# A list-scheduled kernel whose planner supposes later landings and longer hand-overs

## The chip, the cores and the metric

The kernel runs on one core of a Trainium2 chip. The metric is device time in microseconds (us) of one execution. The core has five instruction streams: TensorE (PE, with its weight loads PEld), VectorE (DVE), ScalarE (ACT), GpSimd (POOL) and SyncE (SP), which here issues all loads and transposes by DMA. Engines meet through semaphores only.

## What is computed

Sparse attention, then a feed-forward layer with a softmax-weighted activation and a layer norm. In the reference's terms, cut to what matters:

```python
# q, k, v: 8 batches, 8 heads, 576 positions, 64 wide
scores = (q @ k.T) / 8                       # heads 0-3: the last 32 positions; heads 4-7: every 32nd position
attn = softmax(where(mask, scores, -1e9))
x = (attn @ v) laid out as 4608 tokens x 512
h = x @ w_in                                 # 512 -> 1024
solu = h * softmax(h)
ln = (solu - mean) / sqrt(var + 1e-6) * g_ln
out = ln @ w_out                             # 1024 -> 512
```

Attention inputs are float32. For the large matmuls the kernel splits each operand into two float16 parts, a high and a low one, and adds three products.

## The kernel before

**Tiles and stages.** A *unit* (`unit`, line 322) is one of five pieces of a batch's attention: two for the strided heads, three for the local ones; 40 in all. Its steps are: scores into `s_ps` on TensorE (L341, L346); row maximum, subtraction, exponential, row sum and reciprocal on VectorE and ScalarE (L352 to L361); normalisation on GpSimd (L364, tile `t`); high and low parts on ScalarE and VectorE (L370, L371, tile `p`); a DMA transpose to `pt` (L373); the product with v into `x_ps` on TensorE (L394); and the two parts of x, `xhi` and `xlo` (L410, L411), written to a ring that holds two batches.

An *ff tile* (`ff`, line 415) is 128 tokens through the feed-forward layer; 36 in all. Its steps are: two halves of the first matmul, `g1` (L452 to L454, 12 matmuls each, one PSUM bank each of `h_ps`); the maximum `st` (L459, L460); the exponential `e` (L461); the product `u` (L463) and its mean (L466); the squares (L467); GpSimd's small norms (L471 to L481); the two parts of `c` (L484, L485); a DMA transpose to `ct` (L488); two halves of the second matmul, `g2` (L492 to L494), into `o_ps`; and the scaling and the store (L500, L501).

`h_ps` has three banks. Tile n uses banks 0 and 1, then the next tile 0 and 2, then the next 1 and 2, so one half of the next tile can start while the tile before it still holds its own two banks:

```python
banks, halves = (((0, 1), (0, 1)), ((0, 2), (1, 0)), ((1, 2), (0, 1)))[n % 3]
hv, o, O = h_ps[:, banks[0] : banks[1] + 1 : banks[1] - banks[0]], o_ps, "o"
HH = [("h", i) for i in banks]
```

The two last tiles write `s_ps` in place of `o_ps`, and the last one uses `x_ps` in place of `h_ps`. At the start the weights are decoded, scaled and split (`decode`, `prep_w`, `prep_o`, lines 510 to 575), mostly on VectorE and ScalarE, next to the first units; `v_scale` and `v_split` (lines 278 and 297) do as much for v of each batch.

**What sets the order.** Nothing above is issued where it is written. Each step is handed to a planner, `Plan.add` (line 74), with its engine, a duration in us, a key, and the names that it reads and writes. `Plan.order` (line 92) then runs a list schedule over five simulated engines: whenever an engine is free it takes, among the steps that are ready by the plan's own clock, the one of lowest key. The resulting sequence is the order in which instructions are issued, and so the order in each engine's queue. The plan's times are used for nothing else: on the chip each engine runs its queue in order, and an instruction starts when the semaphores that it needs are there. The waits on the chip are put in from the tiles' accesses in the order of issue.

Keys come from the lists `UK` (units), `TK` (ff tiles, 1.11 per tile), `LK`, `VK`, `LF`, `LW` (loads), `KW` and `KO` (the weights), with small offsets per step. Three constants of `Plan` describe what lies between steps:

- `DMA_LATENCY`: time from the end of a transfer's own duration until its readers are ready. The issue itself is taken as 0.55 us, and transfers follow one another.
- `DMA_AHEAD`: how far SP may run ahead of the transfers.
- `HOP`: time from a step's end until a reader on another engine is ready.

Of the kernel before, what the change touches and what calls it, by code (L numbers as in the profile page):

```python
# [60 lines left out]
class Plan:  # L61
# [1 line left out]

    DMA_LATENCY = 2.0
    DMA_AHEAD = 1.0
    HOP = 0.1

    def __init__(self):  # L70
        self.steps = []
# [20 lines left out]
    def order(self):  # L92
# [15 lines left out]
        while len(out) < len(steps):  # L108
# [12 lines left out]
            if e == "sp":  # L121
                dma_free = max(dma_free, now + 0.55) + dur
                free[e] = max(now + 0.55, dma_free - self.DMA_AHEAD)
                end = dma_free + self.DMA_LATENCY
            else:
# [4 lines left out]
            for m in users[n]:  # L130
                left[m] -= 1
                ready_at[m] = max(ready_at[m], end + (0.0 if steps[m][0] == e else self.HOP))
                if not left[m]:
# [535 lines left out]
```

## Time and profile before

| what | value |
|---|---|
| median of 3 runs | 612.12 us (610.24 to 617.36) |
| the profiled execution's own time | 613.98 us |
| its span in the profile | 612.3 us |
| mean granted TensorE clock | 0.946 |

A page of the profile gives each engine's busy time. A row of waits reads "engine line waited for: us in total, times, longest". A row of the groups of instructions reads "line engine operation output<-input shapes xcount | busy us, mean ns of one | idle us of the engine before them, and what ended it". A row of the timeline reads "start, length, engine, line, operation", with the idle time of the engine before it in brackets. In the chain that ended last a row is "start, length, what", and "issue" is time in which the engine waited for nothing that the profile shows. DMA rows give the count, the size and the median time from issue to landing. Of a window's busy times the last columns are the granted clock of TensorE (PEclk), the share of the DMA engines and GB/s.

### The profile page before, as it was taken

What the parts mean: (1) busy time and instruction counts of PE and PEld (TensorE: products, weight loads), DVE (VectorE), ACT (ScalarE), POOL (GpSimd) and SP (SyncE); (2) the same over time, 40 slices, a digit from 0 to 9 for tenths busy, and PEclk for the clock granted to TensorE, in tenths of its full rate; (3) what the DMA queues carried; (4) which work ended last, traced back from release to release, by engine and by line L of the source; (5) the groups of instructions that cost most, each with busy time, mean ns of one, the idle gap of its engine ahead of it and who ended that gap; (6) DMA issues with size and microseconds to landing.
All of it is one profiled execution on the core that took longest, in us unless ns stands there. A gap on an engine that the chain in (4) does not pass through costs nothing.

```text
span 612.3 us, 11764 instructions
## 1 busy us (share of the span) xinstructions
PE 496.2 (81%) x4808; PEld 254.8 (42%) x4808; DVE 368.5 (60%) x647; ACT 297.6 (49%) x437; POOL 153.7 (25%) x305
## 2 busy tenths in 40 slices
PE   0236925879987899899998999789998889899865
PEld 0233523435444454435454444434454444344322
DVE  3578888866567557666574667476665664333340
ACT  3746536545643565346543464356534453333440
POOL 2020004333222323223322132244222232113130
PEclk9999965989989999879998899799999998999979
DMA  8799587789529983988378847974497554422252
GB/s 320 292 241 280 149 155 206 179 179 233 99 55 205 247 216 78 204 212 201 79 164 199 212 95 171 216 194 114 100 211 125 108 97 82 85 53 52 51 112 59
DMA packets 171157, 96.89 MB, mean 158 GB/s; under 512 B 138208, under 2 KB 157280, under 8 KB 171104
## 3 DMA queue, kind: packets, MB, share of 16 engines
q1 hardware_dynamic: 165920, 86.71, 63.1%
q10 hardware_dynamic: 5184, 9.44, 4.9%
q8 instruction: 37, 0.61, 0.4%
q14 instruction: 16, 0.13, 0.1%
HBM read 39.24 MB, written 9.44 MB: 80 GB/s over the span
## 4 chain that ended last, share of the span: by engine, by line
PE 36%; DVE 23%; ACT 13%; DMA 12%; POOL 8%; issue 7%; ACTq 1%; SPq 0%; DVEq 0%; POOLq 0%
PE h_ps L452 7%; PE h_ps L454 6%; PE h_ps L453 6%; DVE u L463 4%; DMA pt<-p 4%; DVE st L459 4%; PE o_ps L492 4%; ACT e L461 4%; PE o_ps L494 4%; PE o_ps L493 4%; DMA ct<-c 3%; DMA vrl<-vloc 3%; POOL t L364 3%; DVE c L485 2%; PE x_ps L394 2%
## 5 line engine op out<-in xcount | busy, mean ns | idle before, releaser
L452 PE MATMUL h_ps<-w,xhi 128*128 128x512 f16 x280 | 112.5, 402 | 30.3 <-DVE st L459 14.3
L492 PE MATMUL o_ps<-obuf,ct 128*128 128x512 f16 x272 | 104.2, 383 | 11.4 <-DMA ct<-c 11.4
L453 PE MATMUL h_ps<-w,xhi 128*128 128x512 f16 x280 | 112.6, 402 | 0.0
L454 PE MATMUL h_ps<-w,xlo 128*128 128x512 f16 x280 | 112.4, 401 | 0.0
L493 PE MATMUL o_ps<-obuf,ct 128*128 128x512 f16 x272 | 104.0, 382 | 0.0
L494 PE MATMUL o_ps<-obuf,ct 128*128 128x512 f16 x272 | 103.9, 382 | 0.0
L461 ACT ACTIVATE e<-h_ps,st,vsc 128x1024 f32<-128x1024 f32 x31 | 37.3, 1204 | 109.5 <-PE h_ps L454 57.8
L471 POOL TENSOR_SCALAR st<-st 128x1 f32<-128x1 f32 x36 | 10.3, 286 | 293.1 <-DVE st L466 287.7
L364 POOL TENSOR_TENSOR t<-t,m 128x576 f32<-128x576 f32 (+2 forms) x40 | 52.5, 1314 | 122.6 <-DVE m L361 95.9
L463 DVE SCALAR_TENSOR_TENSOR u<-h_ps,e 128x1024 f32<-128x1024 f32 x35 | 42.8, 1222 | 64.0 <-ACT e L461 49.8
L485 DVE SCALAR_TENSOR_TENSOR c<-u,st,c 128x1024 f16<-128x1024 f32 x36 | 47.3, 1315 | 39.9 <-ACT c L484 39.9
L459 DVE TENSOR_REDUCE st<-h_ps 128x1 f32<-128x1024 f32 x35 | 42.5, 1216 | 32.2 <-PE h_ps L454 32.2
L467 ACT ACTIVATE e<-u,st 128x1024 f32<-128x1024 f32 x36 | 41.3, 1147 | 40.8 <-DVE st L466 40.8
L453 PEld LDWEIGHTS <-xhi 128*128 128x128 f16 x288 | 29.3, 102 | 63.1 <-issue 37.4
L484 ACT ACTIVATE c<-u,st 128x1024 f16<-128x1024 f32 x36 | 41.2, 1146 | 26.2 <-POOL st L481 25.3
L492 PEld LDWEIGHTS <-ct 128*128 128x128 f16 x288 | 28.4, 99 | 51.9 <-DMA ct<-c 19.2
L371 DVE TENSOR_TENSOR p<-t,p 128x576 f16<-128x576 f32 (+2 forms) x40 | 30.5, 762 | 26.1 <-ACT p L370 25.8
L454 PEld LDWEIGHTS <-xlo 128*128 128x128 f16 x288 | 29.5, 102 | 38.0 <-issue 7.1
L452 PEld LDWEIGHTS <-xhi 128*128 128x128 f16 x288 | 29.6, 103 | 35.2 <-issue 6.7
L494 PEld LDWEIGHTS <-ct 128*128 128x128 f16 x288 | 28.4, 99 | 34.6 <-issue 1.1
L346 PE MATMUL s_ps<-k,q 64*54 64x54 f32 (+1 forms) x1280 | 41.9, 275 | 0.0
L493 PEld LDWEIGHTS <-ct 128*128 128x128 f16 x288 | 28.4, 98 | 32.0 <-issue 0.8
(125 smaller groups left out, 730.0 us busy)
## 6 DMA issues: line engine op xcount, KB each, us to landing
out<-ob ACTq DMA_DIRECT2D x36, 256.0 KB, 3.4
vrs<-vstr SPq DMA_DIRECT2D x8, 768.0 KB, 6.9
vd<-vs SPq DMA_DIRECT2D x16, 384.0 KB, 5.9
vrl<-vloc SPq DMA_DIRECT2D x8, 640.0 KB, 6.2
q<-qstr SPq DMA_DIRECT2D x8, 594.0 KB, 4.9
k<-kstr SPq DMA_DIRECT2D x8, 594.0 KB, 6.0
q<-qloc SPq DMA_DIRECT2D x8, 576.0 KB, 6.2
k<-kloc SPq DMA_DIRECT2D x8, 576.0 KB, 5.9
```

The costliest lines, as they stand in the source:

```text
L346: nc.tensor.matmul(s_ps[row : row + nq, pair, i * nk : (i + 1) * nk], q_raw[half][hs, q0 : q0 + (nq - 1) * nqb + 1 : nqb], k_raw[half][hs, ...
L364: add("pool", nx * nk / 500 + 0.1, lambda: nc.gpsimd.tensor_tensor(tv, tv, sm.unsqueeze(2).broadcast_to([P, nx, nk]), op=ALU.mult), key + ...
L452: nc.tensor.matmul(hv[:, i], xhi[:, cc, tok], whi[:, cc, cols], start=(cc == 0), stop=False)
L453: nc.tensor.matmul(hv[:, i], xhi[:, cc, tok], wlo[:, cc, cols], start=False, stop=False)
L454: nc.tensor.matmul(hv[:, i], xlo[:, cc, tok], whi[:, cc, cols], start=False, stop=(cc == 3))
L459: add("dve", 1.21, lambda: nc.vector.tensor_reduce(nm, hv, axis=AX.XY, op=ALU.max, negate=True), key + 0.2, r=HH, w=[(ST, "nm")])
L461: add("act", 1.3, lambda: nc.scalar.activation(ev, hv, AF.Exp, bias=nm, scale=hs, accum_out=z), key + 0.25, r=[*HH, (ST, "nm"), *SC], w=[E ...
L463: add("dve", 1.3, lambda: nc.vector.scalar_tensor_tensor(uv, hv, 1.0, ev, op0=ALU.mult, op1=ALU.mult, accum_out=us), key + 0.3, r=[*HH, E] ...
L485: add("dve", 1.35, lambda: nc.vector.scalar_tensor_tensor(c[:, 1], u, r, c[:, 0], op0=ALU.mult, op1=ALU.subtract), key + 0.45, r=[U, (ST, ...
L492: nc.tensor.matmul(o, ct[:, cc, :], ohi[:, cc, :], start=(cc == 0), stop=False)
L493: nc.tensor.matmul(o, ct[:, cc, :], olo[:, cc, :], start=False, stop=False)
L494: nc.tensor.matmul(o, ct[:, 8 + cc, :], ohi[:, cc, :], start=False, stop=(cc == 7))
```

## The change

Two constants of the planner:

```diff
-    DMA_LATENCY = 2.0
+    DMA_LATENCY = 5.0
     DMA_AHEAD = 1.0
-    HOP = 0.1
+    HOP = 0.4
```

Both act in `Plan.order` only: `end = dma_free + self.DMA_LATENCY` for a step of SP (line 124), and `end + HOP` for a reader on another engine (line 132). Steps, durations, keys, buffers and dependencies stay. The same instructions are issued in another order.

## Prediction

> **What bounds the kernel now.** I read the page first (span and engines), then the busy time of three stretches, then TensorE's waits in each.
>
> ```profile
> span 612.3 us, 11764 instructions
> PE 496.2 (81%) x4808; PEld 254.8 (42%) x4808; DVE 368.5 (60%) x647; ACT 297.6 (49%) x437; POOL 153.7 (25%) x305
> ```
> ```profile
> core 0: us, PE busy (x) PEld busy (x) DVE busy (x) ACT busy (x) POOL busy (x), PEclk, DMA share, GB/s
> 0.00:100.00 100.00, 40.62 (x604) 28.19 (x608) 73.32 (x142) 52.28 (x85) 13.19 (x20) 0.91 0.87 246
> 100.00:500.00 400.00, 362.93 (x3686) 185.46 (x3679) 255.86 (x446) 206.42 (x297) 116.38 (x227) 0.95 0.73 159
> 500.00:612.30 112.30, 92.68 (x528) 41.17 (x525) 39.35 (x60) 38.88 (x57) 24.12 (x58) 0.95 0.36 77
> ```
>
> TensorE is the bound from 100 to 500 us (362.93 of 400 busy). Before that VectorE is (73.32 of 100 busy, while it prepares the weights). The last 112 us are TensorE work (92.68) with a latency chain at its end. The change can only move the 612.3 − 496.2 = 116 us in which TensorE idles and the time lost to a low granted clock. The waits, in the same three stretches:
>
> ```profile
> PE s_ps L341 <- DVE t L353: 21.6, 7, 5.2
> PE s_ps L248 <- ACT junk L283: 21.4, 2, 20.4
> ...
> PE h_ps L452 <- DVE st L459: 14.2, 12, 2.6
> PE h_ps L452 <- DVE u L463: 9.0, 9, 1.4
> PE h_ps L452 <- ACT e L461: 6.7, 4, 1.8
> PE x_ps L394 <- DMA pt<-p: 5.6, 6, 2.5
> PE o_ps L492 <- DMA ct<-c: 1.6, 3, 0.6
> ...
> PE o_ps L492 <- DMA ct<-c: 9.8, 4, 5.0
> PE s_ps L492 <- DMA ct<-c: 2.8, 2, 1.5
> ```
>
> The columns are total, times, longest. In the middle the five rows make 37.1 us, of which 29.9 is the first matmul step waiting for a PSUM bank and 7.2 is a transposed tile that has not landed.
>
> **What the change does, and how far the old constants were right.** No instruction is added or removed. The planner walks simulated engines and issues, on each, the step of lowest key that it thinks ready. Readiness now comes 3.0 us later behind every SP transfer and 0.3 us later behind every hand-over to another engine. So only the order in the five queues changes, and engines take their queues in order: a step that is put too early blocks what is behind it, one put too late finds its engine with something else.
>
> Hand-overs first. One feed-forward tile late in the run, with nothing else on the engines (the chain that ended last; start, length):
>
> ```profile
> 535.61 0.23 DVE st L460
> ...
> 535.92 1.30 ACT e L461 x2
> ...
> 537.25 1.25 DVE u L463 x2
> 538.49 0.02 issue
> 538.51 0.16 DVE st L466
> ...
> 540.78 0.73 POOL st L481
> ...
> 541.54 1.16 ACT c L484
> ...
> 542.72 1.30 DVE c L485
> ...
> 544.08 4.38 DMA ct<-c
> ```
>
> VectorE to ScalarE takes 535.92 − 535.84 = 0.08, ScalarE to VectorE 0.03, GpSimd to ScalarE 0.03, ScalarE to VectorE again 0.02. The old 0.1 is near these; 0.4 is 0.3 too much on each. Transfers:
>
> ```profile
> k<-kstr SPq DMA_DIRECT2D x8, 594.0 KB, 6.0
> ...
> pt<-p SPq DMA_TRANSPOSE x40, 4.3
> ct<-c SPq DMA_TRANSPOSE x36, 5.0
> ```
> ```profile
> DMA to landing us min/median/max: 4.2/5.0/8.4
> ```
>
> The planner's sum for ct is 0.55 issue + 2.55 + 2.0 = 5.1 (measured median 5.0), for pt 0.55 + 12 × 0.16 + 2.0 = 4.5 (4.3). With 5.0 they become 8.1 and 7.5: about the worst that is seen (8.4 for ct). For k it is 0.55 + 1.65 + 2.0 = 4.2 against 6.0; the new one says 7.2. So plain loads were taken too early by 1.8 and are now late by 1.2, and the two transposes, which feed TensorE, were right and are now 3 us pessimistic. The Trainium skill (DMA: Bandwidth & Descriptors, "Anatomy of one DMA — SWDGE (gpsimd) path") gives a fixed cost of about 2.0 us for a transfer, almost all of it the write receipt. It speaks for the old constant; the ct and pt rows agree with it only with the planner's own 0.55 and duration on top, and the path that it describes is GpSimd's, not SP's. By it the change is pure pessimism, which is the slower rival below.
>
> **The sum, by stretch.**
>
> Middle, waits on u (9.0 us, 9 times, longest 1.4). The second half of a tile's first matmul needs the bank that u (L463) frees. From the end of the previous half the planner adds four hand-overs (PE, DVE, ACT, DVE, PE), so it now thinks the bank free 4 × 0.3 = 1.2 us later. Almost every one of these waits is within 1.2, so other ready work goes ahead of them where there is any: nothing to 9.0 gained; I take half, −4.5.
>
> Middle, waits on pt and ct (7.2 us, longest 2.5). The margin grows by 3.0 + 2 × 0.3 = 3.6, more than the longest. TensorE will have put another step first; nothing to 7.2 gained, I take −5, near the upper end because the margin covers each.
>
> Middle, waits on st and e (20.9 us, 16 times). These are another thing:
>
> ```profile
> 389.08 0.55 DVE L411 TENSOR_TENSOR xlo<-x_ps,xhi 128x384 f16<-128x384 f32 x1
> 389.54 1.21 DVE L459 TENSOR_REDUCE st<-h_ps 128x1 f32<-128x1024 f32 x1
> ```
> ```profile
> 390.81 0.59 PE L452 MATMUL h_ps<-w,xhi 128*128 128x512 f16 x1 [2.59 <-DVE st L459]
> ...
> 395.46 0.63 PE L454 MATMUL h_ps<-w,xlo 128*128 128x512 f16 x1
> ```
> ```profile
> 396.13 1.21 ACT L461 ACTIVATE e<-h_ps,st,vsc 128x1024 f32<-128x1024 f32 x1 [7.92 <-PE h_ps L454]
> ...
> ACT e L461 <- PE h_ps L454: 52.8, 12, 7.9
> ```
>
> TensorE waits for st of one tile, runs 12 matmuls, and only then does e of a tile start, 5 us after its st ended at 390.75. The planner's dependencies are by bank and know of no such wait. 12 times from 100 to 500 us is about one tile in three, and one in three uses banks 0 and 2 of h_ps with a stride, whose extent covers bank 1. I read it (an inference) as a wait made from the order in which the steps are issued: the next tile's half on bank 1 falls between st and e. Which side it falls on depends on the plan's clock, and all of st, e and u move later against TensorE's own steps. Falling ahead of st it costs TensorE nothing: −20.9 at best. Falling behind u each of 12 waits grows by e and u, 1.30 + 1.25: +31 at worst. No row says which; I take −4, near nothing, on the better side because st, e and u move later.
>
> Clock. The half above took 12 matmuls in 5.3 us: its starts are 0.43 apart where the same matmuls stand 0.22 apart at 548 us (the fence on the end, below). The middle's granted mean is 0.95, so some 0.05 × 363 = 18 us are lost there. The sum so far takes 13.5 of 37.1 us of waits away; a proportional 6.5 would be the most, and I take −3, as short waits go first. The Trainium skill (TensorE: Matmul & The Clock Gate, "What's actually happening") says the clock halves after an idle window of about 3.4 us. Here 2.59 us of waiting stood before a slow stretch, so shorter gaps seem to suffice; by the page alone this term would be nothing.
>
> Start. The 21.4 us wait is fixed: the first scores depend on the scale of the first v, whatever the planner supposes. The 21.6 us on t (L353) are VectorE's order. t comes after a TensorE hand-over and the maximum, so it is now seen later, and a ready preparation step can go ahead:
>
> ```profile
> L371 DVE TENSOR_TENSOR p<-t,p 128x576 f16<-128x576 f32 (+2 forms) x40 | 30.5, 762 | 26.1 <-ACT p L370 25.8
> ...
> L567 DVE SCALAR_TENSOR_TENSOR obuf<-obuf,gs,mt 128x512 f32<-128x512 f32 x8 | 5.6, 745 | 0.0
> ```
>
> One such step of 0.75 ahead of each of seven is +5; none to two: 0 to +10.5. A gain cannot exceed the 21.6 that is waited. I take +5.
>
> End. SP has only transposes left, and TensorE alternates:
>
> ```profile
> 547.30 1.22 DVE L459 TENSOR_REDUCE st<-h_ps 128x1 f32<-128x1024 f32 x1 [3.30 <-PE h_ps L454]
> ...
> 550.20 1.23 DVE L463 SCALAR_TENSOR_TENSOR u<-h_ps,e 128x1024 f32<-128x1024 f32 x1 [1.42 <-ACT e L461]
> ```
> ```profile
> 548.51 0.39 PE L492 MATMUL o_ps<-obuf,ct 128*128 128x512 f16 x1 [1.24 <-DMA ct<-c]
> 548.73 0.38 PE L493 MATMUL o_ps<-obuf,ct 128*128 128x512 f16 x1
> ```
>
> ct lands at 548.5, the bank is free at about 551.5, and the output matmul rightly goes first. In the new plan the bank moves by 1.2 and ct by 3.6 and four hand-overs of its chain (ACT, POOL, ACT, DVE: 1.2) = 4.8, so the 3.0 between them is more than used up and the first matmul would go first: TensorE then waits 3.0 longer, once, as the output matmuls are a tile behind from there on and no longer wait for ct (two or three waits of 1.2, in the 12.6 of this stretch). Bounds +3 × 5 tiles = +15 and −12.6; I take +1.
>
> Total: −4.5 − 5 − 4 − 3 + 5 + 1 = −10.5. The profiled execution took 613.98 (1.7 around its span); 603.5. The median of the three runs is 612.12, 1.9 lower, so **602**.
>
> **Rivals.** *The order hardly matters* (606 to 618, 0.30): keys are the same, steps with one predecessor chain keep their order, and 363 of 400 us in the middle are work. For it: the old constants were right where TensorE depends on them. Against: 3 us is larger than most steps, so many ties turn. Time 612.
>
> *VectorE's preparation is put in the wrong order* (0.25, slower). One mechanism: before 100 us VectorE has 73.32 of 100 us to do and gates the scores. With two late-seen steps overtaken for each of the seven scores, +10.5 in place of +5, and the first tiles with them; if the three gains of the middle also stay at the −4 of the waits on st and e, the end is 612 + 10.5 + 1 − 4 = 620. It decides from two steps per score on; below that the middle pays for it. The page's 2.0 us would make this likelier.
>
> *The false waits between st and e turn over*: part of either side, from −20.9 to +31, hence the width.
>
> **How the numbers follow.** Faster as summed, 0.45 (592 to 606); little changed 0.30; slower 0.25 (618 to 630). A measurement here can tell about 1%, 6 us, from no change. Range: the low end is 602 − 10 (the rest of the u, pt and clock terms: 4.5 + 2.2 + 3.5); the high end is 624, the start at its bound and the false waits a little worse than none. The forecast's own range is 592 to 606.
>
> **What would show it.** Right: in the middle, waits on u, pt and ct fall from 16 us to about 7, TensorE's busy share from 100 to 500 us rises over 0.92, and the granted clock over 0.95; in the start the wait on t grows; in the end one longer wait at h_ps and none on ct until the last three tiles. Wrong: a middle with as much waiting at h_ps as before, its name moved from one row to another, or a share of TensorE in the first 100 us that is well below 40.62.

## The result, and the profile after

The changed kernel takes 568.08 us, the median of 4 runs (566.7 to 571.72), against 611.18 before: a ratio of 0.929 (95% interval 0.921 to 0.938). The forecast was 602, range 592 to 624. The direction was right, the size was four times too small. Ratios here and below compare runs at the usual granted clock alone; one run of one kernel below (the planner told of the whole of h_ps, with landing 5.0) took 721.51 us at a granted clock of 0.74 and is left out of its median.

The page of the changed kernel, span and TensorE:

```profile
span 564.9 us, 11757 instructions
PE 483.6 (86%) x4808; PEld 251.2 (44%) x4808; DVE 367.0 (65%) x647; ACT 297.7 (53%) x437; POOL 158.3 (28%) x305
```

The same instructions keep TensorE busy 12.6 us less, and it idles 81.3 us instead of 116.1. Fixed windows no longer hold the same work, so I cut both runs by work: the middle runs from the 200th to the 1600th of the 1728 large matmuls. Busy time by window (length, engines, granted clock, DMA share, GB/s), before and then after:

```profile
156.00:567.00 411.00, 375.30 (x3507) 187.38 (x3505) 244.90 (x423) 200.07 (x289) 112.60 (x231) 0.96 0.66 143
```
```profile
154.00:525.00 371.00, 360.63 (x3505) 183.23 (x3503) 241.57 (x419) 200.73 (x289) 119.73 (x233) 1.00 0.78 160
```

The start went from 156 to 154, the middle from 411 to 371, the end from 45.3 to 39.9. TensorE's waits in the middle, before and then after:

```profile
PE h_ps L452 <- DVE st L459: 13.4, 11, 2.6
PE x_ps L394 <- DMA pt<-p: 7.2, 6, 2.5
PE o_ps L492 <- DMA ct<-c: 5.1, 5, 2.3
PE h_ps L452 <- DVE u L463: 5.1, 6, 1.4
PE h_ps L452 <- ACT e L461: 4.9, 3, 1.7
```
```profile
PE o_ps L492 <- DMA ct<-c: 4.6, 2, 2.7
PE h_ps L452 <- DVE u L463: 3.8, 4, 1.4
PE h_ps L452 <- ACT e L461: 1.6, 1, 1.6
PE h_ps L452 <- DVE st L459: 0.3, 1, 0.3
```

35.7 us of waits became 10.3 (−25.4), and 375.3 busy became 360.6 (−14.7) as the granted clock rose from 0.96 to 1.00: together the 40 us. After the change, in the end and in the start, the rows that answer to those of the forecast:

```profile
PE s_ps L492 <- DMA ct<-c: 5.8, 2, 4.2
...
PE s_ps L341 <- DVE t L353: 16.8, 6, 6.5
```

ScalarE's wait from 100 to 500 us, 52.8 us before, is now

```profile
ACT e L461 <- PE h_ps L454: 10.7, 4, 6.2
```

### The profile page after: what moved, and what is told of

Same layout as the page of the kernel before. It is cut to its first block, busy times and chain, and to the rows that moved or that the text cites. A ratio compares the mean times of both kernels' runs of the same rounds, so it can differ in the third digit from the quotient of the medians.

```text
span 564.9 us, 11757 instructions
## 1 busy us (share of the span) xinstructions
PE 483.6 (86%) x4808; PEld 251.2 (44%) x4808; DVE 367.0 (65%) x647; ACT 297.7 (53%) x437; POOL 158.3 (28%) x305
## 4 chain that ended last, share of the span: by engine, by line
PE 64%; DMA 14%; DVE 14%; ACT 3%; issue 3%; SPq 1%; ACTq 0%; DVEq 0%
PE h_ps L452 10%; PE h_ps L453 9%; PE h_ps L454 9%; PE o_ps L492 8%; PE o_ps L493 8%; PE o_ps L494 8%; DMA ct<-c 6%; PE x_ps L394 4%; DMA vrl<-vloc 3%; DMA pt<-p 3%; PE s_ps L346 3%; DVE u L463 2%; DVE m L356 2%; DVE c L485 2%; DVE t L353 1%
## 5 line engine op out<-in xcount | busy, mean ns | idle before, releaser
L452 PE MATMUL h_ps<-w,xhi 128*128 128x512 f16 x280 | 107.9, 386 | 11.9 <-DVE u L463 9.0
L453 PE MATMUL h_ps<-w,xhi 128*128 128x512 f16 x280 | 107.6, 384 | 0.0
L454 PE MATMUL h_ps<-w,xlo 128*128 128x512 f16 x280 | 107.4, 384 | 0.0
L364 POOL TENSOR_TENSOR t<-t,m 128x576 f32<-128x576 f32 (+2 forms) x40 | 53.8, 1345 | 150.3 <-DVE m L361 106.3
L459 DVE TENSOR_REDUCE st<-h_ps 128x1 f32<-128x1024 f32 x35 | 42.8, 1222 | 41.5 <-PE h_ps L454 41.5
L471 POOL TENSOR_SCALAR st<-st 128x1 f32<-128x1 f32 x36 | 10.3, 286 | 183.3 <-DVE st L466 173.0
L463 DVE SCALAR_TENSOR_TENSOR u<-h_ps,e 128x1024 f32<-128x1024 f32 x35 | 42.7, 1221 | 23.8 <-ACT e L461 18.2
L467 ACT ACTIVATE e<-u,st 128x1024 f32<-128x1024 f32 x36 | 41.3, 1147 | 21.4 <-DVE st L466 17.7
L492 PEld LDWEIGHTS <-ct 128*128 128x128 f16 x288 | 28.4, 99 | 45.8 <-DMA ct<-c 11.6
L453 PEld LDWEIGHTS <-xhi 128*128 128x128 f16 x288 | 28.4, 99 | 42.2 <-issue 14.3
L411 DVE TENSOR_TENSOR xlo<-x_ps,xhi 128x384 f16<-128x384 f32 (+2 forms) x40 | 25.6, 641 | 30.0 <-ACT xhi L410 30.0
L500 ACT ACTIVATE ob<-o_ps,st 128x512 f32<-128x512 f32 x34 | 23.2, 683 | 40.4 <-PE o_ps L494 40.4
L452 PEld LDWEIGHTS <-xhi 128*128 128x128 f16 x288 | 28.9, 100 | 32.3 <-issue 2.3
```

Source lines behind the costliest of these rows:

```text
L364: add("pool", nx * nk / 500 + 0.1, lambda: nc.gpsimd.tensor_tensor(tv, tv, sm.unsqueeze(2).broadcast_to([P, nx, nk]), op=ALU.mult), key + ...
L452: nc.tensor.matmul(hv[:, i], xhi[:, cc, tok], whi[:, cc, cols], start=(cc == 0), stop=False)
L453: nc.tensor.matmul(hv[:, i], xhi[:, cc, tok], wlo[:, cc, cols], start=False, stop=False)
L454: nc.tensor.matmul(hv[:, i], xlo[:, cc, tok], whi[:, cc, cols], start=False, stop=(cc == 3))
L459: add("dve", 1.21, lambda: nc.vector.tensor_reduce(nm, hv, axis=AX.XY, op=ALU.max, negate=True), key + 0.2, r=HH, w=[(ST, "nm")])
L463: add("dve", 1.3, lambda: nc.vector.scalar_tensor_tensor(uv, hv, 1.0, ev, op0=ALU.mult, op1=ALU.mult, accum_out=us), key + 0.3, r=[*HH, E] ...
```

## The experiments

Every run is told with its ratio to the kernel before on the same chip. "Distance" below is TensorE work, in the planner's durations, that the order of issue puts between a tile's first matmul and its second (g1 to g2), or between a unit's scores and its product with v; it is worked out from the order, not timed. Where a run adds lines to the kernel, its line numbers are shifted by as many (L465 and L477 of the held planner are L452 and L463 here).

### One constant at a time, and a planner that holds the next tile back

Theory A: the halves of the next tile that fall between maximum and exponential cost the time. Theory B: longer supposed delays give each wait a margin.

```diff
-    HOP = 0.1
+    HOP = 0.4          # hop_only;  dma_only: DMA_LATENCY = 5.0 instead
```
```diff
+                if held:  # before_held; after_held: the same with 5.0 and 0.4
+                    ns = [n for n in ns if not tags[n] or tags[n][0] != "g1" or held <= {tags[n][1]}]
```
(`held` holds the tiles whose maximum is issued and whose u is not.)

> HOP 0.4 alone, DMA_LATENCY 2.0. In its order of issue 11 of the 35 tiles on h_ps have a half of the next tile's first matmul between their maximum and their exponential (14 before the change, 5 after). Theory A (the brackets of that kind cost the time, through a wait that the chip makes between all banks of h_ps): little gain, 595 to 608 us. Theory B (the longer supposed delays give every wait a margin, and each constant gives its share): about half of the 43 us, 585 to 595.

> DMA_LATENCY 5.0 alone, HOP 0.1. 11 tiles have such a half between maximum and exponential. Theory A: 595 to 608 us. Theory B: 580 to 595, since 3.0 us of margin on ct and pt is the larger of the two changes.

> The old constants; the planner holds back a tile's first matmul while another tile's maximum is issued and its product u is not. No tile has a half between. Theory A: 575 to 590 us, TensorE's waits on st and e in the middle gone. Theory B: no gain or slower (608 to 625), since the readiness of everything else is supposed as before and a lookahead of one bank is given up.

> The new constants with the same hold: the 5 tiles that are left become 0. Theory A: a little faster than the changed kernel, 558 to 568 us. Theory B: same or slower, 568 to 580, as one bank of lookahead is given up and the margin was already there.

Measured: hand-overs alone 618.45 (1.012, 1.005 to 1.019); landings alone 605.82 (0.990, 0.984 to 0.996); before_held 649.89 (1.063, 1.056 to 1.069); after_held 597.0 (0.976, 0.969 to 0.983). Alone one constant loses and the other gains 1%; together they gain 7%, so shares do not add, against B as it was put. Landings alone lie where A had them; the three others lie outside the ranges of either theory. With no half between maximum and exponential the kernel before is slower and the change still brings 53 us, which speaks against A. The waits of the middle, hand-overs alone, then landings alone, then before_held:

```profile
PE o_ps L492 <- DMA ct<-c: 11.2, 5, 4.7
PE h_ps L452 <- DVE st L459: 10.6, 10, 2.3
PE x_ps L394 <- DMA pt<-p: 6.2, 2, 5.2
```
```profile
PE h_ps L452 <- DVE u L463: 11.3, 8, 3.5
PE h_ps L452 <- ACT e L461: 9.2, 5, 2.6
PE h_ps L452 <- DVE st L459: 8.5, 8, 2.5
PE o_ps L492 <- DMA ct<-c: 2.1, 1, 2.1
```
```profile
PE h_ps L465 <- DVE u L477: 42.8, 15, 5.9
```

Hand-overs alone move waits from the banks to ct; landings alone move them to the banks. The hold was no clean test: it releases the next tile when u is issued, not when it is done, and so makes a new wait of 2.9 us each (42.8 in 15).

### Filler between tiles

Theory C: what counts is how many tiles have 4 us of other TensorE work between their last half and the next tile's first.

```diff
-G2LAG = 0.55
+G2LAG = 2.4                                                        # g2_later_key
-                end = dma_free + self.DMA_LATENCY
+                end = dma_free + (5.0 if dur == 2.55 else self.DMA_LATENCY)  # ct_landing_5
+                end = dma_free + (2.0 if dur == 2.55 else self.DMA_LATENCY)  # after_ct_landing_2, with 5.0 and 0.4
```

> Old constants; only the key of the second matmul (G2LAG) goes from 0.55 to 2.4, so that it yields to both halves of the next tile's first matmul. In the order of issue 28 of 29 middle tiles have at least 4 us of other TensorE work between their last half and the next tile's first (11 before the change, 19 after it, 7 with the hand-overs alone, 12 with the landings alone). Theory C (what decides is how many tiles have such a filler, some 4 us each): 611 less 17 times 4 or so, 535 to 560 us, faster than the changed kernel. Theory B (margin through supposed delays): no gain, 600 to 620, since every supposed delay is the old one.

> Old constants, but 5.0 us of landing time for the 36 transposes of c alone. 19 tiles have a filler of 4 us, as in the changed kernel. Theory C: 565 to 580 us. Theory B: a small part of the gain, 595 to 610, since hand-overs, loads and the transposes of p have no margin.

> Further on the same way: DMA_LATENCY 6.5, HOP 0.55. 4 tiles have a filler of 4 us. Theory C: the gain is lost, 615 to 640 us. Theory B: as fast as the changed kernel or faster, 560 to 575.

> New constants, but the old 2.0 us for the transposes of c. 14 tiles have a filler. Theory C: 590 to 605 us. Theory B: most of the gain stays, 568 to 580, as waits on ct were only 1.6 us in the middle before.

Measured, in this order: the later key 585.96 (0.959, 0.955 to 0.964); ct landing 5.0 584.49 (0.956, 0.952 to 0.961); 6.5 with 0.55 559.13 (0.915, 0.911 to 0.920); ct landing 2.0 598.77 (0.981, 0.976 to 0.986). The last is as C said and the second nearly; both are against B. The third fells C: 4 such tiles and faster than the changed kernel, as B said. The first misses both: it gains 25 us with every supposed delay as before, and falls short of C. Its waits in the middle say why:

```profile
PE x_ps L394 <- DMA pt<-p: 19.0, 9, 4.8
PE h_ps L452 <- DVE u L463: 4.0, 6, 1.2
```

The key cured the banks (23.4 before, 4.0 now) and the product with v, still close behind its scores, took their place.

### What is supposed too early is waited for

Theory D: TensorE waits on the kind of input that the planner supposes early against the others. Theory E: all supposed delays must be long.

```diff
+        HA = [("h", i) for i in range(3)]   # planner_whole_h_ps: st, e and u read HA in the plan
```

> DMA_LATENCY 5.0, HOP 0.1, and the key of the second matmul later (G2LAG 2.4). Theory D (TensorE waits on the kind of input that the planner supposes too early against the others: with the landings alone that was the banks of h_ps, 29 us in the middle, with the later key alone the transposes of p, 19 us): the key takes the wait on h_ps and the landing that on the transposes, middle waits under 12 us, 560 to 572 us. Theory E (every supposed delay must be long, hand-overs too): 580 to 600, as the old hand-overs leave the waits on h_ps.

> Old constants; the planner's maximum, exponential and product of a tile now read all three banks of h_ps, so the next tile's first matmul is supposed ready only after the product, as the chip's waits have it. Theory D: the waits on st, e and u in the middle (23 us before) fall under 10, those on ct and pt stay (12 us) or grow, 585 to 605 us. If the wait on the whole of h_ps is not what is wrong in the plan: 611 or slower.

> New constants with the later key of the second matmul. Theory D: the waits left in the middle (10 us, half of them on ct) fall to about 5, 560 to 568 us. Theory E: no change, 565 to 572.

> Further still: DMA_LATENCY 8.0, HOP 0.7. Theory E: as fast as 6.5 with 0.55 or faster, 552 to 562 us. Theory D: the two stay in proportion, so the middle stays near 370 us for 1400 matmuls, but steps are now put late that the start and the end need; 560 to 580.

Measured, in this order: landing 5.0 with the later key 564.78 (0.924, 0.914 to 0.934); the planner with the whole of h_ps 615.36 (1.013, 1.008 to 1.019); the new constants with the later key 559.6 (0.918, 0.908 to 0.927); 8.0 with 0.7 555.72 (0.910, 0.903 to 0.918). The first needs no longer hand-over, which is against E; its middle has one kind of wait left:

```profile
160.00:528.00 368.00, 360.97 (x3508) 183.21 (x3507) 246.43 (x422) 203.27 (x292) 117.93 (x235) 1.00 0.78 161
```
```profile
PE x_ps L394 <- DMA pt<-p: 7.0, 3, 3.3
```

The planner that knows the real wait on h_ps lost most of it (23.4 us on the banks in the middle before, 2.9 now) and gained others. The time did not fall, so D missed here:

```profile
PE o_ps L494 <- DMA ct<-c: 17.0, 14, 2.7
PE s_ps L341 <- DVE t L353: 10.7, 7, 1.9
PE h_ps L454 <- DVE u L465: 2.9, 1, 2.9
```

The third is 8.5 us faster than the changed kernel, nearly as D said; E had no change. The fourth has the fastest time of all the runs, as E said. Its middle is 368 us, as far down as the others'; its start, 147 us, is the shortest of those compared here, against D's guess that start and end would pay.

### Which landings, and is the order a lucky one

```diff
+        if eng == "sp" and w[0][0] in ("pt", "ct"):
+            self.turns.add(n)
-                end = dma_free + self.DMA_LATENCY
+                end = dma_free + (5.0 if n in self.turns else 2.0)   # loads_5: 2.0 and 5.0 changed over
```

> HOP 0.4; the landing is 5.0 for the transposes to pt and ct alone and 2.0 for all plain loads. Theory D (waits go to what is supposed too early; transposes and hand-overs feed TensorE): nearly all of the gain, 565 to 580 us. If the loads' landing matters as much: 590 to 610.

> The other half: HOP 0.4, landing 5.0 for plain loads alone, transposes 2.0. Theory D: as the hand-overs alone, 605 to 620 us, with the waits on ct and pt (17 us in the middle there). If the loads carry it: 570 to 585.

> A neighbour of the change: DMA_LATENCY 4.0, HOP 0.4. Theory D: waits on transposes partly back, 570 to 588 us. If the changed kernel's order is a lucky one among many: anywhere from 580 to 615.

> The planner told of the wait on the whole of h_ps (615 us with the old constants, where waits on ct took the place of those on h_ps), now with landing 5.0 and HOP 0.1. Theory D: both kinds are now supposed late enough, waits on ct go too, 565 to 585 us. If serial tiles simply cost what the order saves: 605 to 625.

Measured, in this order: the transposes 563.14 (0.924, 0.920 to 0.928); the loads 612.87 (1.005, 1.001 to 1.009); 4.0 with 0.4 581.33 (0.952, 0.947 to 0.957); the planner with the whole of h_ps 625.62 (1.027, 1.021 to 1.033). With HOP at 0.4, all of the gain of the longer landing is in the two transposes; the loads have no part. The transposes at 5.0 with HOP at 0.1 were not run by themselves. The neighbour fits what D said and also a lucky order; but with 4.0 and 0.4, 5.0 and 0.4, 6.5 and 0.55, 8.0 and 0.7 the time falls steadily (581, 568, 559, 556), which speaks against luck. The last is a miss for D: landing 5.0 did not take the waits away once the planner runs tiles one after the other. It still waits:

```profile
PE h_ps L454 <- DVE u L465: 12.6, 8, 4.2
PE o_ps L494 <- DMA ct<-c: 11.3, 5, 5.3
PE s_ps L341 <- DVE t L353: 10.2, 6, 2.1
```

### Distance set by keys alone

Over these kernels the time goes by and large with the two distances (means over tiles 3 to 30 and units 8 to 37, us):

| kernel | median, us | g1 to g2 | scores to product with v |
|---|---|---|---|
| landing 8.0, hop 0.7 | 555.7 | 29.5 | 26.4 |
| landing 6.5, hop 0.55 | 559.1 | 29.3 | 26.9 |
| after, g2 later key | 559.6 | 26.3 | 21.4 |
| transposes 5.0, hop 0.4 | 563.1 | 25.9 | 23.6 |
| landing 5.0, g2 later key | 564.8 | 26.2 | 19.2 |
| after | 568.1 | 26.3 | 22.5 |
| landing 4.0, hop 0.4 | 581.3 | 23.7 | 22.2 |
| ct landing 5.0 | 584.5 | 22.3 | 18.8 |
| g2 later key | 586.0 | 26.0 | 16.1 |
| after_held | 597.0 | 22.8 | 21.8 |
| after, ct landing 2.0 | 598.8 | 20.6 | 22.8 |
| landing 5.0 alone | 605.8 | 22.5 | 21.4 |
| before | 611 | 19.1 | 17.3 |
| loads 5.0, hop 0.4 | 612.9 | 20.7 | 19.5 |
| planner whole | 615.4 | 15.4 | 21.3 |
| hop 0.4 alone | 618.5 | 19.3 | 19.4 |
| planner whole, landing 5.0 | 625.6 | 17.4 | 25.8 |
| before_held | 649.9 | 17.5 | 15.2 |

Theory F: the distance itself is the cause. To test it without any supposed delay:

```diff
-        add("pe", nx * (0.063 if half else 0.095) + 0.1, pv, key + 0.9, r=[PT, *VR], w=X)
+        add("pe", nx * (0.063 if half else 0.095) + 0.1, pv, key + 2.4, r=[PT, *VR], w=X)   # both_keys_later: G2LAG = 2.4 too
```

> Old constants; later keys for both consumers: the second matmul (G2LAG 2.4) and the product with v (key + 2.4 in place of + 0.9). Planned TensorE work between producer and consumer: 25.9 and 26.5 us. Theory F (the distance is the cause): as the changed kernel or faster, 555 to 570 us, and the 19 us of middle waits on pt that the first key alone had are gone. If it takes the later supposed readiness itself: 580 to 590, as with the first key alone.

> Old constants; only the product with v later (key + 2.4). Distances 19.1 (as before) and 26.6. Theory F: the short distance stays and sets the time, 600 to 615 us, waits on pt gone and those on h_ps as before. If either distance gives its share: 585 to 598.

Measured: 564.06 (0.928, 0.920 to 0.936) and 612.54 (1.006, 1.002 to 1.010), both as F said. With the old constants and two later keys the middle is that of the changed kernel:

```profile
157.00:526.00 369.00, 359.98 (x3506) 183.58 (x3504) 249.74 (x422) 200.59 (x291) 113.69 (x235) 1.00 0.80 161
```

With the short distance between the two matmuls left, the middle is as long as before, and the waits are back on banks and ct:

```profile
PE h_ps L452 <- ACT e L461: 16.4, 10, 3.2
PE o_ps L492 <- DMA ct<-c: 11.1, 11, 4.7
```

So, with the old constants throughout, four kernels set the two distances apart: 611 us at 19.1 and 17.3, 586 at 26.0 and 16.1, 613 at 19.1 and 26.6, 564 at 25.9 and 26.5. The cause is shown that far: it is the order, in which TensorE has about 26 us of other work between a tile's two matmuls and some 20 or more between scores and product, and it can be had without any supposed delay. The new constants got it by supposing the transposes and the hand-overs later together; neither alone did. In the traces the margin can be seen directly: over tiles 4 to 30 the second matmul starts 1.4 us (median) after its transpose has landed before the change, 5.2 after it, and 7.7 with both keys later.

The distances do not explain every row. Landing 5.0 alone has 22.5 and 21.4 and is 21 us slower than ct landing 5.0 with 22.3 and 18.8, and the hand-overs alone have both distances longer than before and gain nothing. What else is in those orders stays open, as does why a planner that is told of the whole of h_ps gets worse with later landings, and why it is faster than before_held at a shorter first distance.

## Why the prediction was wrong

**The old constants were called right because they matched the latency.** The step that failed is the judgement that the transposes "were right and are now 3 us pessimistic". As a latency the reading was right: the 5.0 us was the median of the whole run, and over tiles 4 to 30 alone it is 5.0 too, with 4.2 to 8.4 around it. But a consumer that is planned right behind the median landing has nothing left when its own transpose is late. With HOP at 0.4, a landing of 2.0 for the transposes gave 613 (loads at 5.0) and 618 (loads at 2.0); 5.0 for them gave 563. One tile of the kernel before, then one after (maximum, low part of c, landing of its transpose, first of the second matmul):

```profile
458.48 1.21 DVE L459 TENSOR_REDUCE st<-h_ps 128x1 f32<-128x1024 f32 x1
...
470.89 1.28 DVE L485 SCALAR_TENSOR_TENSOR c<-u,st,c 128x1024 f16<-128x1024 f32 x1 [0.97 <-ACT c L484]
```
```profile
DMA to landing us min/median/max: 6.6/6.6/6.6
```
```profile
478.94 0.38 PE L492 MATMUL o_ps<-obuf,ct 128*128 128x512 f16 x1
```
```profile
315.73 1.23 DVE L459 TENSOR_REDUCE st<-h_ps 128x1 f32<-128x1024 f32 x1 [1.24 <-PE h_ps L454]
...
330.22 1.28 DVE L485 SCALAR_TENSOR_TENSOR c<-u,st,c 128x1024 f16<-128x1024 f32 x1
```
```profile
DMA to landing us min/median/max: 4.3/4.3/4.3
```
```profile
343.59 0.38 PE L492 MATMUL o_ps<-obuf,ct 128*128 128x512 f16 x1
```

Before, the chain takes 13.7 us, and the second matmul stands 6.8 us behind the end of c, of which the landing takes 6.6: it starts as soon as its input is there. After, the chain takes 15.8 and the matmul stands 12.1 behind, of which the landing takes 4.3. Over tiles 4 to 30, read the same way, the medians from the end of c to the matmul are 6.8 and 11.6, the least 4.5 and 9.6. The hand-overs (0.02 to 0.08 us) were read from a quiet stretch at the end of the run, where from the maximum's start (534.35) to the end of c (544.02) a tile took 9.7 us; as sizes of single steps they were right. Their use, and that of the median landing, as the measure of how early to place a consumer was not.

**Term by term**, forecast against measured in the middle, cut by work as above. Waits on u: −4.5, measured −1.3. Waits on pt and ct: −5, measured −7.7 (12.3 to 4.6). Waits on st and e: −4, measured −16.4 (18.3 to 1.9): by far the most mis-sized of the waits, taken near nothing because no row gave the side. In the forecast's own stretch (100 to 500 us; after the change the same large matmuls run from 101 to 463.7) the waits on u stay at 9.0, those on pt and ct go from 7.2 to 4.6, those on st and e from 20.9 to 2.8. So the term on u gained nothing there. Of the forecast's signs of being right, TensorE's busy share (347.9 of 362.7 us) and the granted clock (0.98) came; the waits on u, pt and ct together fell only from 16.2 to 13.6. Clock: −3, measured −14.7. It was scaled with a part of the waits, while the slow stretches nearly all went: granted 1.00 in place of 0.96. The kernels whose middles have some 10 us of waits or less are all at about 360 us of TensorE time there and a granted clock of 1.00, so that is its work at full clock. The prediction had written down both bounds that came nearly true, −20.9 for st and e and 18 us of clock, but its range took in neither. That the direction was right is partly luck: the term that moved most among the waits had been given a side without a row for it, with +31 as its other bound.

**The inference on h_ps** was wrong in one point. The wait was read as one tile in three, from the strided banks 0 and 2. By the order of issue it is any tile: 14 of 35 have a half of another tile between maximum and exponential, of all three bank arrangements, and 13 of these 14 exponentials wait for TensorE in the trace. I read the waits as made for the whole of h_ps, so that its third bank gives no free lookahead here. After the change there are 5. That these waits fell is shown; that they are not the whole cause is shown by before_held and by 6.5 with 0.55, which has 13 of them and 5.0 us of waits on st.

**Start and end.** Start: +5 forecast, −2 measured; VectorE's wrong order (the slower rival) did not come, the wait on t went from 21.6 to 16.8. End: +1 forecast, −5.4 measured; the longer wait at h_ps did not come, and the waits on ct from 500 us on (after the change, from the same work on, 463.7) went from 12.6 to 5.8. The sum of the misses: 23.5 in the middle, 7.0 and 6.4 in the start and the end, which is the difference between −10.5 and −47.4 in the span.

**The weighing of the two rules.** The Trainium skill (DMA: Bandwidth & Descriptors, "Anatomy of one DMA — SWDGE (gpsimd) path") was taken to make the change pure pessimism. The rows still agree that a transpose lands about 5 us after its issue. But the true latency was not the right number for the planner. On the clock, the Trainium skill (TensorE: Matmul & The Clock Gate, "What's actually happening") has an idle window of about 3.4 us as the trigger. The trace agrees in the direction only: a wait of 2.59 us, which is shorter, stood before a slow stretch, and the clock's term, which the prediction put at nothing by that section alone, measured −14.7 us.

## What to carry to other kernels

In a list schedule for queues that run in order, a supposed latency is not only a forecast of the latency; it sets the distance between producer and consumer. Here it paid to set it for the slowest instance seen before the change, or beyond, and for every kind of input that the bound engine waits on at once: lengthening one alone moved the wait to the other. When all of one engine's waits are short and of changing names, look at how far its consumers stand behind their producers before looking at any single wait.

## What the runs showed of the hardware

In the middle of the kernel before, 35.7 us of waits, none over 2.6, went with 14.7 us more TensorE time at a granted clock of 0.96; with 10.3 us of waits left the granted mean was 1.00. So short waits were there some 1.4 times as dear as they looked. The price is not fixed: with only the product's key later, 40.8 us of waits went with 9 us more (369.5 busy, granted 0.98).
